# Attention and feed-forward in one kernel: the weight sums moved from the third token tile into the second, with new queue orders

## The chip, the cores and the metric

The kernel runs on one core of a Trainium2 chip. The metric is the time of one execution on the device in microseconds (us); of several runs the median counts. A profile is one further execution, recorded by the hardware.

## What is computed

The input x has 2048 tokens of 512 features. The reference, cut to its core:

```python
xn = _layernorm(x, axis=-1)
q, k, v = (xn @ wqkv).reshape(B, S, 3, H, Dh).transpose(2, 0, 3, 1, 4)      # H = 32, Dh = 16
scores = einsum("bhqd,bhkd->bhqk", q, k) * (Dh ** -0.5)
mask = (i - j >= 0) & (i - j < 256)                                            # sliding window
s = einsum("bhqk,bhkd->bhqd", softmax(where(mask, scores, -1e9)), v).reshape(B, S, D) @ wo
g = silu((silu(xn @ w1) * (xn @ w3)) @ w2)                                     # w1, w3: 512 x 1792
return x + s * g
```

## The kernel before

**Number format.** TensorE multiplies fp16. Each fp32 operand is cut into a high and a low fp16 half (a cast, L1059, and a subtraction, L1060, or the like), and three products of halves stand for one.

**Tiles.** The tokens go in four tiles t = 0 to 3 of 512. The feed-forward part has 14 blocks f of 128 hidden features. For t = 0 and 1, `gate_up` (L1024) multiplies each block by w1 and w3 plainly. For t = 2 and 3 the blocks go in seven pairs j, and `quad(t, j)` makes a pair's 2 x 2 block product with seven multiplications instead of eight, by Strassen's scheme: products p1, p2, p6, p5, p7, p3, p4 in this order, 12 or more matmuls of 256 columns each (L1175). Between them stand pieces of attention, and `down` (L1284), which multiplies by w2.

**What the seven products need.** p1 and p2 take plain weights, which tile 0 left in DRAM as `dW`; p6, p5, p7 and p3 take sums of weight blocks; p6, p5, p7 and p4 take sums of token blocks.

- `weight_sums(j)` makes the sums of pair j, first of w1, then of w3: two loads of 256 KB from HBM (L1073, tensor in_B_w), two scales on ScalarE (L1078), four sums on GpSimd (L1082 to L1085), the cut into halves (L1059, L1060) and two stores of 256 KB to `dSum` (L1094). All seven pairs are made once and are used by both tiles 2 and 3. The pieces are put off by a count of steps (`later`):

```python
for k in range(2):
    n = 8 * k
    later(n, lambda k=k: load(k))
    for i in range(2):
        later(n + 10 + i, lambda i=i, k=k: scale(i, k))
    later(n + 12, lambda k=k: sums(k))
    for i in range(2):
        later(n + 14 + 2 * i, lambda i=i, k=k: cut(i, k))
```

- `token_sums(t)` makes the sums of tile t's tokens on GpSimd (L324, L1125 to L1128), cut into halves in the same way (L1059, L1060).
- `load_quad` brings a pair's plain pieces from `dW` (L1148) and its sums from `dSum` (L1150) back into SBUF, some products ahead of their use.

`QUAD_AT` (L57) says where `feed_forward` starts `weight_sums(j)`: at block f of tile 1, or at pair j of tile 2. `HALVES_AT` (L58) says the same for `token_sums`.

**Behind a product** of a quad: ScalarE copies the bank out (`copied`, L1181) or VectorE adds it to an earlier copy (`added`, L1185); GpSimd multiplies (L1197), ScalarE takes the tangent (L1198), VectorE gates (L1201), and ScalarE and GpSimd cut the result into halves for `down`.

**Attention** in pieces: `pass1` multiplies keys by queries (L652) and VectorE takes row maxima (L665); `pass2` multiplies again (L794), VectorE adds the mask (L800), ScalarE takes the exponential (L802), and TensorE multiplies by the values (L820). `finish` and `normalise` gather the outputs through DMAs (L841, L844, L867, L873) and scale them (L324, L888). `project` makes queries and keys of the next tile (L590, L605, L608, stores L611 to L615), fetched back as KA and qa (L633; the maxima are written into qa by L749).

**What sets the order.** TensorE follows the order in which the code is written. VectorE, ScalarE, GpSimd and SP (which issues nearly all DMAs) follow `QUEUES`: for each engine a list of the numbers of its instructions, laid out by a planner beforehand. `queue` chains them by that list, so each engine runs strictly in this order, and an instruction that waits holds all behind it. `TURNS` adds pairs of a VectorE and a GpSimd instruction of which the first must end before the second starts. Intermediate tiles share 51 slots of SBUF (`take`, `give`), and a new tile waits for the last reader of the old one in its slot. DMAs go out over eight lanes in turn, each waiting for the landing of the one eight places ahead of it.

Of the kernel before, what the change touches and what calls it, by code (L numbers as in the profile page):

```python
# [56 lines left out]
QUAD_AT = ((1, 4), (1, 6), (1, 8), (1, 10), (1, 12), (2, 0), (2, 2))  # L57
# [26 lines left out]
def tile_block(ctx: ExitStack, tc: tile.TileContext, x, wqkv, wo, w1, w3, w2, out):  # L84
# [1302 lines left out]
    def feed_forward():  # L1387

        pieces = []
        late, next_late = [], []  # L1390
        sums_at = dict(zip(QUAD_AT, range(FB // 2)))

# [342 lines left out]
    for n, b in enumerate((1, 3, 0)):  # L1735
# [54 lines left out]
    ),  # L1790
    ENGINE.Activation: (
# [148 lines left out]
```

## Time and profile before

| | |
|---|---|
| median of 3 runs | 793.54 us (793.53 to 795.88) |
| profiled execution, span in it | 799.8 us, 798.0 us |
| granted TensorE clock, mean | 0.998 |
| busy: PE, DVE, ACT, POOL | 779.9, 618.4, 435.1, 398.1 us |
| scales of weights (L1078, 28 of them) | first at 279.0, last at 531.1 us |
| first sums (L1082) of the pairs 0 to 6 | 282.0, 345.7, 356.9, 400.9, 426.0, 458.3 and, of pair 6, after 497.8 us |
| first and last store of sums (L1094) | 288.5 and 561.8 us |
| DMA landing, 256 KB from in_B_w / dW / dSum | 4.5 / 3.8 / 3.6 us after issue (medians) |

Names: PE is TensorE, DVE VectorE, ACT ScalarE, POOL GpSimd, SP or SPq the queue of SyncE; PEld is the loading of weights into TensorE, beside its matmuls. L-numbers are lines of the kernel. A tile's name stands as out<-in: `slot` is any of the 51 tiles, `m` and `s`, `po` are PSUM banks of the feed-forward and of attention, `copy` a quad's copied product, `pt` an exponential. Times count from the span's start. Tile 2 of the feed-forward starts with the first L1181, at 423 us. From 420 to 480 us the queue of SP issues eight loads (L1073) and seven stores (L1094) of 256 KB for the pairs 3 to 5.

### The profile page before, as it was taken

How to read it: one execution, taken by the hardware profiler on the slowest of the kernel's cores; microseconds unless marked ns; L12 is line 12 of the kernel's file. 1: busy time of each engine (PE TensorE's matmuls, PEld its weight loads, DVE VectorE, ACT ScalarE, POOL GpSimd, SP SyncE). 2: the span in 40 equal slices, each digit the busy share in tenths (PEclk: the TensorE clock that was granted, in tenths of full speed). 3: DMA queues.
4: the chain of work that ended last, by engine and by line, in shares of the span. 5: the costliest groups of instructions: out<-in, count | busy, mean ns of one | idle time of the engine just before them, and what ended most of it. 6: DMA issues, size and time to landing. Idle time of an engine off the chain costs nothing.

```text
span 798.0 us, 25742 instructions
## 1 busy us (share of the span) xinstructions
PE 779.9 (98%) x9997; PEld 443.5 (56%) x9997; DVE 618.4 (78%) x2049; ACT 435.1 (55%) x672; POOL 398.1 (50%) x761
## 2 busy tenths in 40 slices
PE   8999999999999999999998789999999999999998
PEld 4444555444455544444446566566666666666654
DVE  8788998777987688777778687767887788876456
ACT  7899768644365444354444466554555445555421
POOL 2264556453323082089996387454883315142451
PEclk9999999999999999999999999999999999999999
DMA  9867672366746545486787875469655666344333
GB/s 305 258 186 254 174 226 69 114 178 226 218 143 187 163 122 142 140 198 204 224 257 220 232 240 154 144 205 269 188 168 179 185 180 180 106 138 139 103 100 121
DMA packets 130123, 144.40 MB, mean 181 GB/s; under 512 B 19472, under 2 KB 87888, under 8 KB 130000
## 3 DMA queue, kind: packets, MB, share of 16 engines
q1 hardware_dynamic: 129712, 142.23, 59.9%
q8 instruction: 78, 1.28, 0.7%
q10 hardware_dynamic: 288, 0.52, 0.2%
q14 instruction: 45, 0.37, 0.2%
HBM read 100.40 MB, written 37.49 MB: 173 GB/s over the span
## 4 chain that ended last, share of the span: by engine, by line
PE 78%; DMA 7%; POOL 4%; DVE 4%; SPq 4%; issue 2%; ACT 1%; DVEq 0%; ACTq 0%; POOLq 0%
PE m L1284 16%; PE m L1024 15%; PE m L1175 14%; PE m L590 8%; PE po L820 7%; PE m L1333 4%; PE s L794 3%; PE m L555 3%; PE s L652 3%; DMA slot<-in_B_w_dram 2%; POOL slot L324 1%; DVE copy L1185 1%; DMA KA<-dK 1%; SPq L749 1%; POOL slot L1060 1%
## 5 line engine op out<-in xcount | busy, mean ns | idle before, releaser
L802 ACT ACTIVATE pt<-s,es 128x1024 f32<-128x1024 f32 x130 | 142.2, 1112 | 75.5 <-DVE s L800 69.7
L1284 PE MATMUL m<-slot,slot 128*128 128x512 f16 x672 | 153.4, 379 | 0.9 <-DVE copy L1185 0.3
L324 POOL TENSOR_TENSOR slot<-slot,slot 128x256 f16<-128x256 f32 (+1 forms) x136 | 91.6, 691 | 121.4 <-ACT slot L1050 56.1
L665 DVE CUSTOM_DVE_ANT_0 junk<-s,MW 128x320 bf16<-128x320 f32 x276 | 127.0, 485 | 12.8 <-PE s L652 5.9
L1024 PE MATMUL m<-XH,slot 128*128 128x512 f16 x448 | 133.6, 380 | 0.0
L1175 PEld LDWEIGHTS <-slot 128*128 128x128 f16 x1176 | 113.0, 98 | 30.3 <-issue 6.0
L800 DVE TENSOR_TENSOR s<-s,MK 128x256 f32<-128x256 f32 (+1 forms) x236 | 99.0, 435 | 38.9 <-PE s L794 34.4
L1284 PEld LDWEIGHTS <-slot 128*128 128x128 f16 x672 | 63.7, 98 | 75.9 <-issue 4.7
L1024 PEld LDWEIGHTS <-slot 128*128 128x128 f16 x672 | 62.9, 98 | 76.3 <-issue 3.5
L1024 PE MATMUL m<-XL,slot 128*128 128x512 f16 x224 | 84.9, 379 | 0.0
L1175 PE MATMUL m<-slot,slot 128*128 128x256 f16 x672 | 81.0, 273 | 3.0 <-DVE copy L1185 1.7
L1197 POOL TENSOR_TENSOR copy<-copy 128x256 f32<-128x256 f32 x56 | 41.4, 743 | 84.6 <-DVE copy L1185 70.9
L665 DVE CUSTOM_DVE_ANT_0 junk<-po,MW 128x320 bf16<-128x320 f32 x172 | 82.1, 483 | 0.0
L820 PE MATMUL po<-pt,V 64*32 64x320 f32 (+4 forms) x2880 | 78.2, 342 | 2.2 <-issue 2.2
L1181 ACT ACTIVATE copy<-m 128x512 f32<-128x512 f32 x56 | 33.4, 597 | 84.5 <-PE m L1175 75.8
L340 POOL TENSOR_TENSOR slot<-slot,slot 128x128 f16<-128x128 f32 x112 | 45.5, 436 | 59.9 <-ACT slot L337 58.9
L590 PE MATMUL m<-XH,slot 128*128 128x512 f16 x240 | 70.7, 380 | 0.2
L820 PEld LDWEIGHTS po<-pt,V 64*32 64x32 f32 x2880 | 53.8, 106 | 21.5 <-issue 3.9
L1175 PE MATMUL m<-XH,slot 128*128 128x256 f16 x336 | 58.0, 277 | 2.8 <-DMA slot<-dW 2.8
L590 PEld LDWEIGHTS <-slot 128*128 128x128 f16 x392 | 36.8, 98 | 41.5 <-issue 1.6
L794 PEld LDWEIGHTS <-KA 50*64 50x64 f16 x1472 | 33.6, 106 | 35.4 <-issue 26.8
L1185 DVE SCALAR_TENSOR_TENSOR copy<-m,copy 128x512 f32<-128x512 f32 x42 | 29.0, 690 | 30.9 <-PE m L1175 30.7
(198 smaller groups left out, 1403.7 us busy)
## 6 DMA issues: line engine op xcount, KB each, us to landing
slot<-dW SPq DMA_DIRECT2D x112, 256.0 KB
slot<-in_B_w_dram SPq DMA_DIRECT2D x70, 256.0 KB
slot<-dSum SPq DMA_DIRECT2D x56, 256.0 KB
dW<-slot SPq DMA_DIRECT2D x42, 256.0 KB
slot<-in_A_x_dram SPq DMA_DIRECT2D x30, 256.0 KB
dSum<-slot SPq DMA_DIRECT2D x28, 256.0 KB
KA<-dK SPq DMA_DIRECT2D x24, 288.0 KB
slot<-dWQ SPq DMA_DIRECT2D x24, 256.0 KB
```

Of the source, the lines that this page charges most:

```text
L324: op(out[:, c], a[:, c], b[:, c])
L340: nc.gpsimd.tensor_sub(lo[:, c // 2, at], raw[:, c * P:(c + 1) * P], hi[:, c // 2, at])
L590: nc.tensor.matmul(cell["pp"][:, cols[n]], w[:, (a * NC + c) * P:(a * NC + c + 1) * P], b[:, c, cols[n]], start=n == 0 and (c, i) == parts ...
L665: nc.vector.tensor_tensor_reduce(out=junk, in0=view, in1=mask, scale=1.0, scalar=NEG, op0=ALU.add, op1=ALU.max, accum_out=M[:, r, a, ii:ii ...
L794: nc.tensor.matmul(s[64 * h:64 * h + 64, r, o:o + 64 * n], ka[rows, 2 * p + a, 64 * (m + 4):64 * (m + 5)], qa[rows, 2 * p + a, 64 * (m + k ...
L800: nc.vector.tensor_add(v, v, MK[:, kind, of:of + n, :].unsqueeze(1).to_broadcast([P, 2 * len(which), n, 64]))
L802: nc.scalar.activation(pt, s, AF.Exp, scale=es)
L820: nc.tensor.matmul(cell["po"][32 * i:32 * i + 32, h, 64 * (m + k):64 * (m + k + n)], V[64 * h:64 * h + 64, (4 * t + m // 2) % VB, hd * VW: ...
L1024: nc.tensor.matmul(cell[k], w[:, at:at + P], b[:, c, :], start=c == 0 and i == 0, stop=c == NC - 1 and i == 2)
L1175: nc.tensor.matmul(ps[:, 256 * k:256 * k + 256], w(k, a, c), x(b, c), start=first and k == 0 and c == 0 and n == 0, stop=k == 1 and c == 1 ...
L1197: nc.gpsimd.tensor_mul(made[:, 256:512], made[:, 0:256], made[:, 256:512])
L1284: nc.tensor.matmul(ps, hh[:, a * TW + b * P:a * TW + (b + 1) * P], w[:, c * D:(c + 1) * D], start=f == f0 and i == 0, stop=f == f1 - 1 and ...
```

## The change

Each pair's sums are started earlier, all within tile 1: pair 0 at its block 1 instead of 4, pair 6 at its block 13 instead of pair 2 of tile 2. `HALVES_AT` stays. The lists of `QUEUES` for all four engines and the pairs of `TURNS` are new throughout, since the numbers of the instructions change with the order of the code. The numbers of instructions are the same.

```diff
-QUAD_AT = ((1, 4), (1, 6), (1, 8), (1, 10), (1, 12), (2, 0), (2, 2))
+QUAD_AT = ((1, 1), (1, 3), (1, 5), (1, 7), (1, 9), (1, 11), (1, 13))
...
 QUEUES = {
     ENGINE.DVE: (
...
-        "0 4 2 1 3 5-9 11 10 12 18-22 13 23-24 14 25 15 26 16 27 17 28-33 35 38 34 37 39 44 40-42 45 47 50 46 48 52-53 "
...
+        "0 4 2 1 3 5 7 6 8-9 11 10 12 18-22 13 23-24 14 25 15 26 16 27 17 28-33 35 38 34 37 39 44 40-42 45 47 50 46 51 "
...
 TURNS = (
-    "240-88 241-90 242-104 255-104 204-104 224-105 205-105 225-105 206-106 226-112 227-94 243-97 244-99 298-122 "
...
+    "198-70 255-108 204-112 205-92 224-113 206-95 243-93 244-97 225-84 227-124 268-125 269-131 271-130 311-148 "
...
```

What the lists do at three places, as the built programs have it. First SP, at the opening of tile 2. Before (`slot_8246` is a plain weight piece of the second quad of tile 2; another, `slot_8141`, stands four rows ahead of these):

```order
L633 DMA qa<-dQ_148 48x4x512 x2
L1150 DMA slot_8265<-dSum 128x1024
L1094 DMA dSum<-slot_7087 128x1024
L1073 DMA slot_7704<-in_B_w_dram 128x4x128
L622 DMA slot_8216<-dWQ 128x1024
L615 DMA dK_153<-slot_8235 128x512
L614 DMA dK_153<-slot_8235 128x2x512
L749 DMA qa<-mt 1x8x128 x2
L844 DMA on<-os 16x512
L749 DMA qa<-mt 1x8x128
L844 DMA on<-os 16x512 x3
L1148 DMA slot_8246<-dW_155 128x2x512
```

Now (the same two pieces are `slot_8319` and `slot_8208`):

```order
L612 DMA dQ_148<-slot_7818 128x512
L873 DMA rb<-de 16x512 x2
L1148 DMA slot_8319<-dW_155 128x2x512
L633 DMA KA_144<-dK_152 48x4x768 x2
L633 DMA qa<-dQ_148 48x4x512 x2
L1148 DMA slot_8208<-dW_155 128x2x512
L841 DMA dr<-os 64x1x32
L1094 DMA dSum<-slot_7525 128x1024
L1094 DMA dSum<-slot_7367 128x1024
L1094 DMA dSum<-slot_7585 128x1024
L1073 DMA slot_7808<-in_B_w_dram 128x4x128
L1150 DMA slot_8335<-dSum 128x1024
```

The piece that stood behind the gathers L844 now stands ahead of the fetches of KA and qa (L633), and the other behind them. The gathers come after all of these rows, and so does the load L1150 that stood next to L633 (on `slot_8265` before, `slot_8337` now).

Second ScalarE, around the first copy of a product in tile 2. Before (slot_7513 and slot_7512 are weights of pair 4):

```order
L802 ACTIVATE pt<-s,es_334 128x1024
L1181 ACTIVATE copy<-m_8030 128x512
L1078 ACTIVATE slot_7513<-slot_7513,inv 128x512
L1078 ACTIVATE slot_7512<-slot_7512,inv 128x512
L1198 ACTIVATE slot_8071<-copy,sga 128x256
L802 ACTIVATE pt<-s,es_334 128x1024 x2
L802 ACTIVATE pt<-po,es_334 128x1024
L1181 ACTIVATE copy<-m_8030 128x512
```

Now (slot_7182 and slot_7181 are weights of pair 5):

```order
L1078 ACTIVATE slot_7182<-slot_7182,inv 128x512
L802 ACTIVATE pt<-s,es_334 128x1024
L1038 ACTIVATE slot_7900<-m_7887,sgs 128x512
L1050 CAST slot_7917<-slot_7900 128x512
L802 ACTIVATE pt<-s,es_334 128x1024
L1078 ACTIVATE slot_7181<-slot_7181,inv 128x512
L1181 ACTIVATE copy<-m_8102 128x512
L802 ACTIVATE pt<-s,es_334 128x1024 x2
L802 ACTIVATE pt<-po,es_334 128x1024
L1181 ACTIVATE copy<-m_8102 128x512
L802 ACTIVATE pt<-s,es_334 128x1024
```

The two scales and the tangent L1198 that stood between the first copy and the exponentials are gone from there; scales of the next pair stand ahead of the copy.

Third VectorE, at the second quad's addition of a product (the last row before, the middle one now). Before:

```order
L665 ISA junk,M<-s,MW 128x320
L665 ISA M 128x1
L665 ISA junk,M<-s,MW 128x320
L665 ISA M 128x1
L665 ISA junk,M<-po,MW 128x320
L665 ISA M 128x1
L513 TENSOR_TENSOR XL<-s,XH 128x2x128
L665 ISA junk,M<-po,MW 128x320
L665 ISA M 128x1
L1185 SCALAR_TENSOR_TENSOR copy<-m_8686,copy 128x512
```

Now:

```order
L665 ISA junk,M<-po,MW 128x320
L665 ISA M 128x1
L665 ISA junk,M<-po,MW 128x320
L665 ISA M 128x1
L464 TENSOR_SCALAR slot_7077<-slot_7077,mv,rs 128x512
L1185 SCALAR_TENSOR_TENSOR copy<-m_8738,copy 128x512
L800 TENSOR_TENSOR s<-s,MK 128x4x64
L665 ISA junk,M<-s,MW 128x320
L665 ISA M 128x1
L800 TENSOR_TENSOR s<-s,MK 128x2x2x64
```

The addition stood behind the masks, the maxima and the cut (L513) of a group of scores; now it stands ahead of them, behind a LayerNorm pass (L464) of tile 3, which came earlier in the list before.

On GpSimd, the cuts of the token sums of tile 2 (L1059, L1060 on `slot_7488` and `slot_7513`, read by p6, p5 and p7) now stand among the last sums and cuts of pair 5, ahead of the first product L1197 of a quad; the sums of pair 4 stood there before. Pair 6 follows behind that L1197, with its loads on SP behind the rows shown.

247 rows, old and new, of tables (QUEUES, TURNS) are left out of this document.

## The prediction

> **What bounds the kernel now.** I read the busy shares first, then TensorE's idle time by stretches, its waits, and the timeline at each place where it stood. First TensorE on the page; then stretches (length, busy time and instructions of PE, PEld, DVE, ACT, POOL, then granted clock, DMA share, GB/s).
> ```profile
> PE 779.9 (98%) x9997; PEld 443.5 (56%) x9997; DVE 618.4 (78%) x2049; ACT 435.1 (55%) x672; POOL 398.1 (50%) x761
> 240.00:340.00 100.00, 99.68 (x1424) 50.73 (x1423) 75.62 (x247) 45.02 (x60) 32.00 (x56) 1.00 0.52 152
> 340.00:420.00 80.00, 79.56 (x974) 38.72 (x979) 59.46 (x200) 39.35 (x49) 75.30 (x132) 1.00 0.77 222
> 420.00:440.00 20.00, 17.93 (x262) 12.51 (x247) 17.25 (x54) 8.79 (x13) 12.52 (x27) 1.00 0.76 215
> 440.00:460.00 20.00, 15.67 (x297) 11.53 (x295) 13.94 (x48) 8.61 (x15) 6.81 (x13) 0.91 0.84 243
> 460.00:480.00 20.00, 17.36 (x351) 11.89 (x349) 16.68 (x50) 12.68 (x23) 16.59 (x27) 1.00 0.73 227
> 520.00:540.00 20.00, 19.14 (x204) 12.58 (x210) 12.77 (x43) 11.46 (x16) 12.40 (x21) 1.00 0.73 213
> ```
> TensorE is the bound, and the change leaves its work as it is: the same rows, but for one group of nine matmuls that changes places with a projection near 385 us. What can be won is idle time. Of 798.0 − 779.9 = 18.1 us, 2.07 + 4.33 + 2.64 = 9.04 lie in 420 to 480, the opening of tile 2, and 0.86 in 520 to 540. The stretch of 440 to 460 also shows a clock of 0.91. From 240 to 420 TensorE was idle for 0.32 + 0.44 = 0.76 us only.
>
> Its waits, by what ended them (total, times, longest):
> ```profile
> PE m L1175 <- DMA slot<-dW: 2.8, 1, 2.8
> PE po L820 <- issue: 2.2, 2, 1.3
> PE m L1175 <- DVE copy L1185: 1.7, 1, 1.7
> PE m L1175 <- ACT V L557: 0.8, 1, 0.8
> ```
> The 2.2 us of "issue" wait for nothing that the profile shows; the other three follow below. All these are of the profiled execution: 799.8 us, 1.8 of it outside the span, and 6.3 above 793.54, the median of the runs. I make the sum in the profiled execution and take the same difference off the median; that some of its stalls may be the profile's own is in the range.
>
> **Place A, 428.7 to 431.3: exponentials late on ScalarE.** TensorE's timeline, then ScalarE's and VectorE's (start, duration, what, idle before):
> ```profile
> 427.26 1.47 PE L1175 MATMUL m<-slot,slot 128*128 128x256 f16 x12
> 429.27 0.42 PE L794 MATMUL s<-qa,KA 50*64 50x320 f16 x12 [0.53 <-ACT pt L802]
> 430.27 0.29 PE L652 MATMUL s<-KA,qa 48*64 48x320 f16 x1 [0.58 <-ACT pt L802]
> 431.28 0.29 PE L652 MATMUL po<-KA,qa 48*64 48x320 f16 x1 [0.71 <-ACT pt L802]
> 425.15 0.72 ACT L1078 ACTIVATE slot<-slot,inv 128x512 f32<-128x512 f32 x1 [1.36 <-DMA slot<-in_B_w_dram]
> 427.10 0.72 ACT L1078 ACTIVATE slot<-slot,inv 128x512 f32<-128x512 f32 x1 [1.22 <-DMA slot<-in_B_w_dram]
> 428.13 2.10 ACT L802 ACTIVATE pt<-s,es 128x1024 f32<-128x1024 f32 x2
> 425.19 1.02 DVE L800 TENSOR_TENSOR s<-s,MK 128x512 f32<-128x512 f32 x2
> ```
> The masks (L800) of the first exponential (L802) were done by 426.2, yet it started at 428.13, behind two scales of pair 4 (L1078) that stood 1.36 + 1.22 us for weights from HBM. TensorE lost 0.53 + 0.58 + 0.71 = 1.82. The change takes these scales, and the tangent behind them, out of the way: after the first L1181 the exponentials come next, up to 1.9 us earlier, which covers each gap. I take 1.5 (0 to 1.8; a scale of pair 5, on slot_7181, now stands one place ahead of L1181 and can itself be late).
>
> **Place C, 449.0 to 455.5: a weight piece for the second quad's next product.** The load's issue, its flight in the chain of waits, and TensorE's restart:
> ```profile
> 444.55 2.47 SPq L844 DMA_DIRECT2D on<-os  x3
> 447.12 4.95 DMA slot<-dW
> 452.12 0.60 PE L1175 MATMUL m<-XH,slot 128*128 128x256 f16 x2 [2.82 <-DMA slot<-dW]
> 452.12 2.74 PE m L1175 x12
> 464.59 1.47 PE L1175 MATMUL m<-slot,slot 128*128 128x256 f16 x12 [1.72 <-DVE copy L1185]
> 434.26 0.87 SPq L633 DMA_DIRECT2D KA<-dK  x2
> ```
> The 256 KB landed 4.95 us after issue, and the issue stood behind three gathers (L844). Twelve matmuls then took 2.74 us, where others take 1.47: half clock. A clock of 0.91 over 20 us is 0.09 × 20 / 0.5 = 3.6 us at half speed, so at most 1.8 us of work is lost by it; I take 1.4 (at least the 2.74 − 1.47 = 1.27 shown). In the new SP order this load stands ahead of the fetches of KA and qa (L633), so it goes out before 434.3 and lands by 439.2, ten microseconds ahead of use. Gain 2.8 + 1.4 − 0.2 for new neighbours = 4.0 (2.5 to 4.5).
>
> The Trainium skill ("TensorE: Matmul & The Clock Gate", Part 1: The HAM clock gate) says that the clock falls to half after an idle window of some 3.4 us and comes back after as long a stretch of work. The trace agrees in the half and roughly in the length (3.6), but it fell after gaps of 1.34 and 2.82 us, neither of them so long. By the rule a new stall under 3.4 us would cost nothing beside itself; by the row it can cost 1.27 more, which is what I use.
>
> **Place D, 462.9 to 464.6: 1.72 us for one VectorE addition** (L1185), which stood behind masks, a cut and row maxima (L665, 485 ns below):
> ```profile
> 463.11 0.42 DVE L513 TENSOR_TENSOR XL<-s,XH 128x256 f16<-128x256 f32 x1
> 463.85 0.69 DVE L1185 SCALAR_TENSOR_TENSOR copy<-m,copy 128x512 f32<-128x512 f32 x1
> L464 DVE TENSOR_SCALAR slot<-slot,mv,rs 128x512 f32<-128x512 f32 x16 | 8.5, 566 | 0.0
> ```
> It now stands ahead of two masks (0.5 each, from 1.02 for two), four maxima and the cut: 1.0 + 1.9 + 0.4 = 3.3 us less of VectorE ahead of it; two passes L464 put in front take back 1.1. That covers 1.72: gain 1.4 (0 to 1.7).
>
> **Place E, 531.6 to 532.4: 0.8 us** behind two scales of pair 6:
> ```profile
> 530.47 1.34 ACT L1078 ACTIVATE slot<-slot,inv 128x512 f32<-128x512 f32 x2 [1.29 <-DMA slot<-in_B_w_dram]
> ```
> These scales now stand among ScalarE's rows of 440 to 485. Gain 0.8 (0.5 to 0.9). The two gaps of "issue" I leave as they are: 0. Together 1.5 + 4.0 + 1.4 + 0.8 = 7.7 us.
>
> **What the move costs.** The work of the pairs is not less, only earlier. Prices of its parts on GpSimd (345 to 420):
> ```profile
> L1060 POOL TENSOR_TENSOR slot<-slot,slot 128x256 f16<-128x256 f32 x32 | 21.2, 671 | 0.5
> L1059 POOL CAST slot<-slot 128x256 f16<-128x256 f32 x32 | 12.5, 396 | 0.1
> L1082 POOL TENSOR_TENSOR slot<-slot 128x256 f32<-128x256 f32 x6 | 4.3, 724 | 0.3 <-ACT slot L1078 0.3
> ```
> A pair is 8 sums of 0.724, 8 casts of 0.396 and 8 subtractions of 0.671: 14.3 us, and 8 transfers of 256 KB. Three pairs were made after 420; now six are cut ahead of the first tangent's product (L1197, 431.26 below), so GpSimd takes on about two pairs, 28.7 us, in 240 to 431. Its row of 32.00 in 100 us shows room early; 75.30 of 80 shows none late. TensorE doesn't see early work as long as no operand it needs is cut late.
>
> One such operand I can place: the token sums for product 6 of the first quad, read from 427.26 on (place A). GpSimd's timeline, and the row of SP's queue near which a weight load is now issued:
> ```profile
> 415.25 1.92 POOL L324 TENSOR_TENSOR slot<-slot,slot 128x256 f16<-128x256 f32 x3
> 417.83 2.56 POOL L1060 TENSOR_TENSOR slot<-slot,slot 128x256 f16<-128x256 f32 x4
> 425.95 0.73 POOL L1082 TENSOR_TENSOR slot<-slot 128x256 f32<-128x256 f32 x1 [5.56 <-ACT slot L1078]
> 431.26 0.72 POOL L1197 TENSOR_TENSOR copy<-copy 128x256 f32<-128x256 f32 x1
> 415.36 1.40 SPq L749 DMA_DIRECT2D qa<-mt  x2
> ```
> Before, GpSimd had them by 420.4 and then stood idle. Now the last of them is cut behind three of the four last sums of pair 5. From the second of the three L324, near 415.9, to that cut's end are 17 instructions of 0.39 to 0.73, 10.6 us: 426.5 if no load is late. But the last load of pair 5 stands in SP's new order just ahead of the qa writes of 415.36; issued near 415 and landing 3 to 6 us later (4.95 at C), it holds the sums, behind which 6.7 us are left, until 419 to 422: cut at 426 to 429. Cost 0 to 2 us, taken 0.7.
>
> A load of sums for the second quad (L1150) stood on SP at 436.20, and now stands ten DMAs later, behind the gathers:
> ```profile
> 436.20 0.39 SPq L1150 DMA_DIRECT2D slot<-dSum  x1
> ```
> That is near 445, landing near 450; use was at 455 (after C's twelve) and comes near 449 when A and C are gone: 0 to 2, taken 0.7. Another weight piece on SP (L1148, slot_8208) now waits for GpSimd to be done with pair 5, with everything behind it on SP; it is read only after 440: 0 to 1, taken 0. In 240 to 420 the scales of two more pairs stand in ScalarE's queue ahead of exponentials, as at A: each late load can cost what A cost, 1.8, or nothing, and the idle 0.76 us of that stretch says that the slack there was ample: 0 to 4, taken 0.8. The costs sum to 2.2.
>
> Does a busier GpSimd slow VectorE? Row maxima with GpSimd at 32 of 100, then at 75.3 of 80 us:
> ```profile
> L665 DVE CUSTOM_DVE_ANT_0 junk<-s,MW 128x320 bf16<-128x320 f32 x44 | 20.2, 485 | 5.0 <-ACT XH L508 3.8 <-PE s L652 1.2
> L665 DVE CUSTOM_DVE_ANT_0 junk<-s,MW 128x320 bf16<-128x320 f32 x38 | 17.7, 486 | 2.9 <-PE s L652 2.9
> ```
> By 1 ns: cost 0. The Trainium skill ("SBUF — State Buffer", SBUF: two separate sides) speaks against the change here: a VectorE instruction with two SBUF inputs and one of GpSimd lock each other out. The maxima read one operand from PSUM, so these rows don't test it; by the rule each L1328 (two tiles in SBUF) between 240 and 420 could wait up to 0.7 us, and the sum would change by tenths, since it stands on no wait above.
>
> **The sum:** 7.7 − 2.2 = 5.5 us: 794.3 for a profiled execution, 788.0 as the median.
>
> **Rivals.**
> - Almost all is won: costs come to 0.5, and one gap of "issue" (1.3) goes, with fewer transfers beside it. 7.7 + 1.3 − 0.5 = 8.5: 785.0, at best 782. For it: 420 to 480 loses some seven of fifteen transfers for sums, and 14 us on GpSimd. Against it: "issue" names no transfer. Chance 0.23.
> - No change; the wait only changes its place. Product 6 waits 2 for its token sums, L1150 is 2 late, early scales cost 0.8, C gains its low end 2.5 and D nothing: 1.5 + 2.5 + 0.8 − 4.8 = 0: 793.5, within the 2.4 us (0.3%) that a measurement of this kernel can tell from no change. For it: GpSimd at 75.3 of 80 ahead of product 6. Chance 0.14.
> - Slower: GpSimd falls behind before 427. The two pairs more fit only into the early room (68 us idle in 240 to 340); if loads and free slots let less than half of the 28.7 us be done there, 14 us are late at 427. TensorE stands for them, less the 5.6 us that GpSimd idled at 420 to 426, plus 1.3 of clock: 9.7 lost against 7.7 won, 795.5. It decides from some 12 us of lateness. Against it: a fifth of that room is enough. Chance 0.12.
> - My forecast, a gain of 2.4 to 8: chance 0.51, alone 785.5 to 791.
>
> The range takes in the first rival's end, 782.0, and the slower one's 795.5. Faster 0.74, same 0.14, slower 0.12.
>
> **What will show it.** Right: no wait of L1175 on slot<-dW and a clock of 1.00 in 440 to 460 (C); L802 within 0.5 us of its masks near 426 (A); no L1175 wait on L1185 near 463 (D); no L1078 near 530 (E); some 6 us more of TensorE busy in 420 to 480. Wrong: L1175 waiting for GpSimd's L1060 near 427 or for dSum near 450, or more than 2 us of idle TensorE in 240 to 420, where ScalarE or GpSimd would stand for an early load.

## The result and the profile after

| | before | after |
|---|---|---|
| median | 793.87 us (5 runs, 793.53 to 798.16) | 788.40 us (5 runs, 788.05 to 788.87) |
| ratio | | 0.9917, 95% interval 0.9891 to 0.9943 |
| profiled execution, its span | 799.8, 798.0 us | 788.5, 786.7 us |
| TensorE busy, rest of the span | 779.9, 18.1 us | 777.8, 8.9 us |

The change gains 5.5 us (6.5 against 794.9, the median of 35 further runs of the kernel before). It does something else besides: the five runs after lie within 0.8 us of each other, while 102 further runs of the kernel before lay between 792.0 and 800.4. The granted clock alone is not the gain: of those 102, the 53 with a mean clock of 0.999 or 1.000 still took 794.5 us in the median. The ratios below are those on record with their 95% intervals; they are not the quotients of the two medians and can differ from these by up to 0.14%.

The same stretches and waits of TensorE after (columns as in the prediction), with one stretch of before that was not shown, the last of the five:
```profile
240.00:420.00 180.00, 180.00 (x2430) 90.40 (x2436) 136.29 (x453) 90.59 (x118) 132.73 (x233) 1.00 0.68 202
420.00:440.00 20.00, 19.76 (x262) 13.55 (x251) 17.97 (x60) 10.15 (x14) 14.41 (x32) 1.00 0.88 263
440.00:460.00 20.00, 18.84 (x394) 14.55 (x378) 18.34 (x60) 11.36 (x20) 10.32 (x17) 1.00 0.70 220
460.00:480.00 20.00, 19.73 (x359) 14.32 (x358) 16.05 (x52) 14.47 (x22) 14.85 (x25) 1.00 0.55 165
500.00:560.00 60.00, 59.06 (x768) 37.12 (x766) 44.07 (x148) 32.39 (x46) 29.64 (x49) 1.00 0.68 204
...
PE po L820 <- issue: 0.6, 1, 0.6
PE s L794 <- ACT pt L802: 0.5, 1, 0.5
PE m L1175 <- DVE slot L608: 0.2, 1, 0.2
```
In 420 to 480 the idle time fell from 9.04 to 0.24 + 1.16 + 0.27 = 1.67 us, the clock is 1.00 throughout, and of the four waits that the prediction took up, three are gone and the gap of issue is 0.6 instead of 2.2. From 240 to 420, where GpSimd now works for 132.7 us instead of 107.3, TensorE has no idle time at all.

The places one by one after: ScalarE, VectorE and TensorE at A; SP's issue of C's weight piece; GpSimd's cut of the token sums, and their first use (the row of 426.26); SP's late load of sums (L1150):
```profile
424.96 2.13 ACT L802 ACTIVATE pt<-s,es 128x1024 f32<-128x1024 f32 x2 [2.18 <-DVE s L800]
424.18 1.02 DVE L800 TENSOR_TENSOR s<-s,MK 128x512 f32<-128x512 f32 x2
427.66 0.42 PE L794 MATMUL s<-qa,KA 50*64 50x320 f16 x12
427.09 0.42 SPq L1148 DMA_DIRECT2D slot<-dW  x1
423.15 1.29 POOL L1060 TENSOR_TENSOR slot<-slot,slot 128x256 f16<-128x256 f32 x2
426.26 1.47 PE L1175 MATMUL m<-slot,slot 128*128 128x256 f16 x12
444.32 0.43 SPq L1150 DMA_DIRECT2D slot<-dSum  x1
```
The exponentials now wait for their masks and for nothing else. The weight piece goes out 20 us earlier than at 447.12. The last token sum is cut at 424.4, 1.8 us ahead of use. L1150 goes out at 444.3, as worked out, and no matmul waits for dSum.

### The profile page after: what moved, and what is told of

Same layout as the page of the kernel before. It is cut to its first block, busy times and chain, and to the rows that moved or that the text cites. A ratio compares the mean times of both kernels' runs of the same rounds, so it can differ in the third digit from the quotient of the medians.

```text
span 786.7 us, 25767 instructions
## 1 busy us (share of the span) xinstructions
PE 777.8 (99%) x9997; PEld 443.5 (56%) x9997; DVE 615.3 (78%) x2049; ACT 435.9 (55%) x672; POOL 399.0 (51%) x761
## 4 chain that ended last, share of the span: by engine, by line
PE 94%; DVE 3%; ACT 2%; issue 1%; DMA 1%; SPq 0%; DVEq 0%; ACTq 0%
PE m L1284 19%; PE m L1024 19%; PE m L1175 15%; PE m L590 9%; PE po L820 9%; PE m L555 5%; PE m L1333 5%; PE s L652 4%; PE s L794 4%; DVE copy L1185 1%; ACT pt L802 1%; PE po L652 1%; PE s L500 1%; PE s L590 1%; DMA slot<-in_A_x_dram 1%
## 5 line engine op out<-in xcount | busy, mean ns | idle before, releaser
L802 ACT ACTIVATE pt<-s,es 128x1024 f32<-128x1024 f32 x130 | 142.4, 1112 | 85.1 <-DVE s L800 77.0
L1175 PEld LDWEIGHTS <-slot 128*128 128x128 f16 x1176 | 112.6, 98 | 24.0 <-issue 3.7
L1197 POOL TENSOR_TENSOR copy<-copy 128x256 f32<-128x256 f32 x56 | 41.8, 749 | 101.6 <-DVE copy L1185 89.4
L1175 PE MATMUL m<-slot,slot 128*128 128x256 f16 x672 | 80.9, 273 | 0.5 <-DVE slot L608 0.2
L820 PE MATMUL po<-pt,V 64*32 64x320 f32 (+4 forms) x2880 | 77.7, 342 | 0.6 <-issue 0.6
L820 PEld LDWEIGHTS po<-pt,V 64*32 64x32 f32 x2880 | 54.1, 106 | 19.0 <-issue 1.7
L1175 PE MATMUL m<-XH,slot 128*128 128x256 f16 x336 | 56.9, 273 | 0.0
```

Source lines behind the costliest of these rows:

```text
L802: nc.scalar.activation(pt, s, AF.Exp, scale=es)
L820: nc.tensor.matmul(cell["po"][32 * i:32 * i + 32, h, 64 * (m + k):64 * (m + k + n)], V[64 * h:64 * h + 64, (4 * t + m // 2) % VB, hd * VW: ...
L1175: nc.tensor.matmul(ps[:, 256 * k:256 * k + 256], w(k, a, c), x(b, c), start=first and k == 0 and c == 0 and n == 0, stop=k == 1 and c == 1 ...
L1197: nc.gpsimd.tensor_mul(made[:, 256:512], made[:, 0:256], made[:, 256:512])
```

## The experiments

Numbers in the lists of `QUEUES` are those of the instructions in code order. Each kernel ran beside the kernel before on the same chip.

### A second profile of the kernel before

No edit. 

> The kernel before, unchanged, once more with a profile. Its profiled execution took 799.8 us, 6.3 above its median, while that of the changed kernel took 788.5, its median. Theory 1: most executions of the kernel before lack a part of the stalls of 420 to 480 us (the half clock, the two gaps of issue), and a profile of such an execution shows a span near 792, a clock of 1.00 in 440 to 460 and 3 to 6 us less idle TensorE in 420 to 480. Theory 2: the profile itself lengthens this kernel, and the span is near 798 again with the same gaps.

Measured: 795.92 us in the median of 12 (794.28 to 798.87); the profiled execution took 795.9. Stretches and gaps of TensorE in 420 to 480:
```profile
420.00:440.00 20.00, 19.50 (x244) 13.28 (x241) 18.33 (x57) 10.59 (x15) 14.09 (x31) 1.00 0.78 213
440.00:460.00 20.00, 15.51 (x304) 11.90 (x286) 14.98 (x49) 10.29 (x18) 8.45 (x14) 0.91 0.73 221
460.00:480.00 20.00, 18.98 (x354) 12.56 (x354) 16.16 (x48) 13.67 (x23) 17.32 (x30) 1.00 0.69 216
...
444.93 0.88 PE L820 MATMUL po<-pt,V 64*32 64x128 f32 x28 [2.31 <-issue]
449.43 0.39 PE L1175 MATMUL m<-XH,slot 128*128 128x256 f16 x2 [0.98 <-DMA slot<-dW]
460.75 1.47 PE L1175 MATMUL m<-slot,slot 128*128 128x256 f16 x12 [1.72 <-DVE copy L1185]
```
The stalls are not the same ones. Place A, 1.82 us in the first profile, is gone (0.50 us idle in 420 to 440); C's wait is 0.98 instead of 2.82, the gap of issue 2.31 instead of 1.34; D's 1.72 is the same. Theory 1 holds in part: there are 3.0 us less idle time in 420 to 480, but the half clock stays, and the span is 794.1 us, not near 792. The 799.8 us of the first profile were one end of a spread, and which place stalls changes from one execution to the next.

### One place mended at a time

```diff
 A, Activation: ... 359
-353 351 360-363
+360-363 353 351
 ... 364
 C, SP: ... 561 551 573
+572
 ... 557-560 574 ... 552-554
-572
 ... 564; load_quad(2, 1, 1) gets a tile of its own, and cpool 6 buffers instead of 7
 D, DVE: ... 958
+977
 ... 978-981 983 982 984
-977
 ... 994
```
C needs the tile of its own: its slot of SBUF holds halves that two stores (L614 and L615 in the SP rows ahead of the prediction) still read until 445.7 us, so moved alone it would wait on SP for stores that stand behind it. The smaller ring of copies has a run of its own below.

A: 

> The kernel before, with the two scales of pair 4 moved behind the three exponentials on ScalarE (place A alone). Theory 1, the terms of the prediction add up: 1.5 us faster (792.0). Theory 2, A's gain is swallowed: TensorE then comes earlier to the weight piece of place C, which lands at the same time, so the wait there grows by what A gave and the time stays within 0.5 us of 793.5.

C: 

> The kernel before, with the weight piece of place C issued ahead of the fetches of KA and qa, into a tile of its own (its slot is in use until a store lands near 445.7); to make room for it the ring of copies has 6 tiles instead of 7. Theory 1 (place C costs 2.8 us and 1.4 of half clock in every execution): 4 us faster, 789.5, no wait on slot<-dW. Theory 2 (a typical execution pays the wait but no half clock): 2.5 to 2.8 faster, 791. Theory 3: next waits (row maxima, sums) take it back: under 1 us.

D: 

> The kernel before, with VectorE's addition of place D moved ahead of the masks and maxima of its group of scores (place D alone). Theory 1: 1.4 us faster, 792.1. Theory 2: the maxima that are now 0.7 us later hold a later product as long, and the time stays within 0.5 us of 793.5.

Measured: A 795.97 us, ratio 1.0011 (0.9994 to 1.0027); C 795.04, 0.9994 (0.9976 to 1.0011); D 795.48, 0.9999 (0.9981 to 1.0017); before 794.92 (35 runs). None gains anything that can be told. The intervals exclude the prediction's 1.5 us for A and 4.0 for C; for D they reach a gain of 1.5, so that its 1.4 is not excluded. TensorE's gaps, A first, then C, then D (A's profiled execution took 798.5 us, near the top of its twelve):
```profile
443.72 0.68 PE L500 MATMUL s<-identf,slot 64*32 64x64 f32 x32 [2.62 <-DVE slot L464]
471.10 1.96 PE L820 MATMUL po<-pt,V 64*32 64x320 f32 x40 [2.12 <-issue]
...
445.69 0.55 PE L820 MATMUL po<-pt,V 64*32 64x128 f32 x28 [1.89 <-issue]
452.40 0.41 PE L794 MATMUL s<-qa,KA 50*64 50x320 f16 x8 [1.01 <-ACT pt L802]
459.87 1.47 PE L1179 MATMUL m<-slot,slot 128*128 128x256 f16 x12 [1.72 <-DVE copy L1189]
...
448.59 0.39 PE L1175 MATMUL m<-XH,slot 128*128 128x256 f16 x2 [2.87 <-DMA slot<-dW]
465.20 0.33 PE L652 MATMUL s<-KA,qa 48*32 48x320 f16 x8 [0.76 <-ACT pt L802]
```
(In C's kernel and the later ones with its tile, lines behind 1144 are four further down.) Each mended wait is gone from its own profile (A's was gone from the second profile of before as well), and TensorE stands elsewhere: at L464 and issue with A mended, at issue and L802 with C, at C's load, as before, and newly at L802 with D. By the times, theory 2 holds for A and D and theory 3 for C. The mechanism expected for A does not: C's wait did not grow, it is not in that profile, and L464 came in its place.

The control for the ring: 

> The kernel before with the ring of copies of 6 tiles instead of 7, nothing else: the control for the early weight piece, which needed that room and came out at 795.0 beside 794.9 before. Theory 1 (the waits of 420 to 480 stand one behind the other, and taking away one only lengthens the next): no difference, within 1 us of before. Theory 2 (the smaller ring costs what the early piece gives): 2 us or more slower.

Measured: 794.01 us, 0.9991 (0.9976 to 1.0006). The smaller ring costs nothing, so it did not hide a gain of C.

### The four places at once, and a fifth

```diff
 A, C and D as above
 E, Activation: ... 443
-423 421 444-445
+444-445 423 421
```


> The kernel before with places A, C, D and E mended at once in its own order of sums: the two scales of pair 4 behind the exponentials, the weight piece early in a tile of its own (6 copies in the ring), the addition ahead of its masks, the two scales of pair 6 behind L557. Theory 1 (the four terms of the prediction, 7.7 us, are the gain, whatever makes them): 787 to 789. Theory 2 (the loads and stores of the pairs in 420 to 480 make TensorE late in ever new places, and only their removal helps): 793 or more, with the gap of issue near 444 still 1 to 2.5 us and waits for L464 or L802 in place of those mended.

Measured: 795.46 us, 1.0010 (0.9994 to 1.0026). That is theory 2's time, with its wait for L464; the gap of issue that it named near 444 is missing (0.4 us at 468 is all). TensorE's gap, then GpSimd's rows that lead to it, then VectorE's:
```profile
443.78 0.68 PE L500 MATMUL s<-identf,slot 64*32 64x64 f32 x32 [3.26 <-DVE slot L464]
429.22 0.73 POOL L1082 TENSOR_TENSOR slot<-slot 128x256 f32<-128x256 f32 x1 [9.45 <-ACT slot L1078]
438.71 1.31 POOL L1060 TENSOR_TENSOR slot<-slot,slot 128x256 f16<-128x256 f32 x2
439.97 0.21 POOL L452 TENSOR_TENSOR sq<-r 128x4 f32<-128x4 f32 x1
442.57 0.20 POOL L461 TENSOR_TENSOR rs<-sq,r 128x4 f32<-128x4 f32 x1
442.81 1.79 DVE L464 TENSOR_SCALAR slot<-slot,mv,rs 128x512 f32<-128x512 f32 x2 [3.62 <-POOL rs L461]
```
GpSimd makes the scale of tile 3's LayerNorm (L452 to L461) behind the sums and cuts of pair 4, and these wait for the scales that A moved back. What ScalarE gave to the exponentials, GpSimd lost, and TensorE's transposes (L500) paid 3.3 us for it. This is no rare execution: all twelve show a mean clock below 0.999, as only 49 of the 102 of the kernel before do. So the way in which A is mended costs something itself, and this run doesn't show what C, D and E would give without it. Hence the next edit, which takes pair 4's sums out of GpSimd's way too:
```diff
 A, C, D and E as above
 G, Pool: ...
-473-474 485 475 483 486 484 497 476 422 421 458 457 460 459 477 479 478 480 461-470
+497 422 421 458 457 460 459 461-470 473-474 485 475 483 486 484 476 477 479 478 480
```


> The kernel before with A, C, D and E mended as in the run that came out at 795.5, and with the twelve GpSimd instructions of pair 4's first half (L1082 to L1085 and the cuts, 7.9 us) moved behind the chain L452 to L461. That chain gives the LayerNorm of tile 3 (L464), for which TensorE's transposes (L500) waited 3.3 us in that run. Theory 1 (GpSimd's queue at the opening of tile 2 was the fifth wait, hidden behind the others): the wait at L500 is gone and the time is 788 to 790. Theory 2 (late landings find ever new places as long as the pairs' transfers run there): 792 or more.

Measured: 800.24 us, 1.0060 (1.0034 to 1.0086): slower, outside both theories. TensorE's gap, then SP's and GpSimd's rows behind it:
```profile
450.83 0.64 PE L794 MATMUL s<-qa,KA 50*64 50x256 f16 x8 [5.77 <-DMA qa<-mt]
430.90 0.92 SPq L633 DMA_DIRECT2D qa<-dQ  x2
440.36 0.34 SPq L1154 DMA_DIRECT2D slot<-dSum  x1
439.01 1.31 POOL L1060 TENSOR_TENSOR slot<-slot,slot 128x256 f16<-128x256 f32 x2
```
The wait at L500 is gone, as theory 1 had it. But the next load of sums (L1150, here L1154) goes into slot 38, in which pair 4's raw weights lie until GpSimd has cut them at 440.3. SP stood for it from 431.8 to 440.4, and the maxima that it writes into qa behind it came 5.8 us late. So in this order pair 4 can't go earlier, its loads land too late, and it can't go later, its slots are needed. The new plan has it out of the way altogether.

### Lighter loads and sums, in the old order

```diff
+                n = 1 if j in (4, 5) else NC
-                nc.sync.dma_start(raw.rearrange("p (c f) -> p c f", f=P),
-                                  w[:, f * P:(f + 1) * P].rearrange("(c p) f -> p c f", p=P))
+                nc.sync.dma_start(raw.rearrange("p (c f) -> p c f", f=P)[:, 0:n, :],
+                                  w[:, f * P:(f + 1) * P].rearrange("(c p) f -> p c f", p=P)[:, 0:n, :])
...
             raw = cell[k][i]
-            nc.scalar.activation(raw, raw, AF.Copy, scale=inverses[:, j, k, i:i + 1])
+            src, dst = raw, raw
+            if j in (4, 5):
+                src = identf.unsqueeze(1).to_broadcast([P, NC, P])
+                dst = raw.rearrange("p (c f) -> p c f", f=P)
+            nc.scalar.activation(dst, src, AF.Copy, scale=inverses[:, j, k, i:i + 1])
...
             a, b = cell[k]
+            w = 16 if j in (4, 5) else 256
+            l, r = slice(0, w), slice(256, 256 + w)
```
The first of three kernels has the loads light, the second the sums too (the last two lines), and the third the places A, C, D, E and G besides. The first:

> The kernel before with the sixteen loads... of pairs 4 and 5 (eight of them, L1073, in 420 to 470 us) cut to a quarter of their bytes, 64 KB each; their scales read a constant instead, so these two pairs' sums are not those of the weights. Order, instructions and waits stay. Theory 1 (bytes in flight between 420 and 470 make the landings late: A's scales, C's piece, instruction fetches): 3 us or more faster, 790 to 792, and the runs lie closer together. Theory 2 (it is the order of the queues and the slots, not the bytes): within 1 us of before.

(Eight loads are meant.) Measured: 793.23 us (791.14 to 798.57), 0.9993 (0.9974 to 1.0011).

The second: 

> The kernel before with the eight loads of pairs 4 and 5 at a quarter of their bytes (as before, their scales read a constant) and their sixteen GpSimd sums (L1082 to L1085) on 16 columns instead of 256, so that these pairs' sums are not those of the weights. Order and waits stay. Theory 1 (bytes and GpSimd time between 420 and 470 are what the change removes, and what it gains by): 789 to 791. Theory 2 (order and slots alone bind, since the light loads alone gave at most 1.6 us): 792.5 or more, with the gaps at L1185 and L464 as before.

Measured: 793.67 us (790.53 to 798.75), 0.9986 (0.9964 to 1.0008).

The third: 

> Both at once: the five places mended in the order before, and the loads and sums of pairs 4 and 5 light (their sums are not those of the weights). Theory 1 (places and loads together are all of the change's gain): 787.5 to 789, runs within 1.5 us of each other as those of the changed kernel. Theory 2 (something else in the new plan gives a part, in 0 to 420 or after 500): 790 or more.

Measured: 797.78 us, 1.0033 (1.0017 to 1.0050).

For the first two, theory 2 holds: neither the bytes of pairs 4 and 5 nor the time of their sums on GpSimd give the change's 5.5 to 6.5 us. A part of it is not excluded: the medians lie 1.6 and 0.9 us below those of the kernel before (794.83 and 794.53), and the intervals allow gains up to 2.1 and 2.9. With both light, TensorE still waited 2.32 us for C's piece and 1.7 at D (its line 1182 is L1175); the last line is of the third kernel:
```profile
446.42 0.61 PE L1182 MATMUL m<-XH,slot 128*128 128x256 f16 x2 [2.32 <-DMA slot<-dW]
...
PE m L1182 <- DVE copy L1192: 1.7, 1, 1.7
...
PE s L794 <- DMA qa<-mt: 3.9, 1, 3.9
```
The third run does not test its theory 1. It holds edit G, which alone had made the kernel slower, and SP stood again for the slot that G keeps in use, from 432.9 to 440.0, so the maxima in qa came 3.9 us late. Light loads and sums took 2.5 us off the run with G (800.24 to 797.78). A, C, D and E with light loads and without G were not run.

### The changed kernel with one part put back

C's piece late on SP:
```diff
 SP: ... 505 503
-582
 ... 569-573 564 ... 576-577
+582
 ... 584
```


> The changed kernel with the weight piece of place C (L1148, slot_8319) issued 31 DMAs later on SP, behind the writes of qa near 443.6 us, so that it lands near 448.5 where TensorE wants it at 445.3. Theory 1 (a wait of 3 us on an otherwise gapless TensorE costs itself and a half clock behind it, as the profile of before showed): 3.2 + 1.4 = 4.6 slower, 793.0, clock 0.91 in 440 to 460. Theory 2 (the wait alone, clock 1.00): 3.2 slower, 791.6. Theory 3 (later work has slack that gives it back): under 1 us slower.

(It is 23 DMAs.) Measured: 790.51 us in the median of 12, from 788.48 to 795.28; 0.9954 (0.9935 to 0.9973) against before. Slower by 2.1 in the median, between theories 2 and 3, for in the profiled execution, which is the fastest, SP had reached the load by 442.0 and the wait was short:
```profile
442.00 0.45 SPq L1148 DMA_DIRECT2D slot<-dW  x1
445.06 0.39 PE L1175 MATMUL m<-XH,slot 128*128 128x256 f16 x2 [0.28 <-DMA slot<-dW]
```
What this run shows is the spread. One load issued just in time, in a plan with few other gaps, turned five runs within 0.8 us of each other into twelve runs 6.8 us apart. The granted clock of each run is on record and splits them: the six at 0.999 or 1.000 took 788.5 to 790.6 us, the six at 0.996 to 0.998 took 790.4 to 795.3. So a half clock, as in theory 1, came in some executions and not in others; where in the span it came, a mean doesn't say. That the landing's own scatter decides it is the likely reading; the slow executions have no profile.

Half a pair of sums back into the opening:
```diff
 Pool: ... 388
-493 485 494 507 505 495 506 508 486-487 497 488 498 496 501 503 502 504 533
+485-487 497 488 498 533 493-494 507 505 495 506 508 496 501 503 502 504
 ... 454
```


> The changed kernel with one half pair of sums put back to where GpSimd made sums before: the twelve instructions of pair 5's second half (L1082 to L1085, their cuts L1059 and L1060, 7.9 us) are moved from ahead of the first L1197 to behind it, into the opening of tile 2. Nothing else is moved. Theory 1 (the change gains because GpSimd's queue, and through the slots SP's, is free at the opening): GpSimd reaches L452 near 439 instead of 435, L464 comes 4 us later and TensorE's L500 waits some 3 us; the weight piece in the slot of these sums and all behind it on SP go out 4 to 5 us later; 3 to 6 us slower than the changed kernel, 791.5 to 794.5, and its runs spread by over 2 us. Theory 2 (the gain comes from the four places A, C, D and E by their order alone, with GpSimd off the path): under 1 us slower, 788 to 789.4.

Measured: 788.96 us in 4 runs (788.51 to 789.04), 0.9913 (0.9897 to 0.9930) against before: theory 2's time. GpSimd's first and last row of the half pair, and the start of the LayerNorm chain:
```profile
424.99 0.73 POOL L1082 TENSOR_TENSOR slot<-slot 128x256 f32<-128x256 f32 x1
430.47 1.31 POOL L1060 TENSOR_TENSOR slot<-slot,slot 128x256 f16<-128x256 f32 x2
435.60 0.20 POOL L452 TENSOR_TENSOR sq<-r 128x4 f32<-128x4 f32 x1 [0.51 <-DVE r L437]
```
Eight us of sums in the opening cost nothing that can be told: 788.96 against 788.40 us, measured in different series, and 0.9913 against 0.9917 of the kernel before. The weights were there: GpSimd did these sums from 425.0 to 431.8 without a wait and still stood for VectorE (L437) before L452. In the kernel before it idled 5.56 us for pair 4's scales ahead of such work. This points to the wait for loads issued at 421, and not to GpSimd's work at the opening; half a pair is all that was put back. Theory 2's cause, the four places by their order alone, does not follow from its time: mended in the old order they gained nothing.

### What follows

In the kernel before, weights issued at 421 met an opening in which ScalarE, GpSimd, SP and the slots were each close to holding TensorE. Shown are: that the places A, C and D one by one, and all four with E, give no gain in the old order that can be told; that lighter transfers and sums give, by their interval, 2.9 us at most; that mending A moves the wait to L464 through GpSimd, and mending that moves it to SP through a slot; and that with the loads early, a half pair of sums at the opening is nearly free. Not tried are C, D and E without A, the four places with light loads and without G, the old plan with its loads alone issued earlier, and the new places with late sums; the last two need queue orders planned anew. What makes the gain of the new plan, the earlier sums or the rest of it, therefore stays open.

## Why the prediction was right, and where it wasn't

The time, 788.0 against 788.4, and the side were right. The way there was right in part.

- **Places A, C, D, E.** All four waits are gone from the profile after, with the half clock, as said. But the step "together 1.5 + 4.0 + 1.4 + 0.8 = 7.7 us" took them as terms that stand by themselves and come in every execution. In the second profile of the kernel before A's wait was absent and C's was 0.98 us, so A's and C's terms were sized by one execution at the slow end. Mended one by one or together in the old order they give nothing that can be told: mending A makes GpSimd late, and another wait comes in its place.
- **C's cause.** The step "the issue stood behind three gathers" named the nearer half. The slot, held by stores until 445.7, bound it as well, and the change helped by giving the piece another slot (slot 2, free by 427).
- **The gaps of issue.** "I leave as they are: 0" was mis-sized: 2.2 became 0.6, so 1.6 us more.
- **The costs.** "The costs sum to 2.2" was mis-sized: they were 0. The token sums were cut at 424.4 (worked out: 426 to 429), L1150 went out at 444.3 and nothing waited for it, and TensorE's idle time in 240 to 420 went from 0.76 to 0.00 instead of growing by 0.8. GpSimd had no idle load to wait for ahead of the cut, so the risk on which the two cautious rivals stood didn't come to bear.
- **The base.** "Take the same difference off the median" was the weakest step. The profiled execution moved by 799.8 − 788.5 = 11.3 us, twice the 5.5 of the sum: 9.2 us of idle time (7.4 in 420 to 480, 0.8 in 240 to 420, 0.6 in 500 to 560, 0.5 in the first 20) and 2.1 of busy time, most of it half clock. The 794.3 us given for a profiled execution was 5.8 too high. But the execution of before that was profiled lay 6.3 above its median, and the median moved by 5.5. Too small a gain and too slow a base cancelled; that the forecast came within 0.4 us of the result is luck.

The half clock went with its waits, as the step had it; it was priced at 1.4, and TensorE's busy time fell by 2.1. The gap of 1.34 us, which the prediction named beside C's, had no part in it (last section).

## What to carry to other kernels

Where a tuned kernel's bound engine shows several short waits close together on different releasers, they are probably ends of parallel chains with little slack, and their sum is gained only by a change that relieves the chains; mending one wait shows the next. A load issued a few microseconds ahead of its use cost 2.1 us in the median here and much more in the spread, so move it early, and check whose slot it needs. Compare profiles with the median first, and profile the kernel before twice: a spread of 1% between its executions says that the one profile's stalls are not the typical ones.

## What was not expected of the hardware

- **Instruction fetch.** The gap of issue at L820 came in most profiles, and by the trace's packet records TensorE resumed 1.25 to 1.46 us after a 16 KB packet of the instruction queue had landed (before: landed 446.02, resumed 447.33; its second profile 443.63 and 444.93; C mended 444.45 and 445.69; D mended 442.47 and 443.76; after 442.01 and 443.47). It stands where some 130 short matmuls (L500, L820) run in 2.9 us, and is long where the packet starts late. What makes it start late wasn't tried.
- **Half clock after short gaps.** The clock of 440 to 460 was 0.91 after gaps of 1.34 and 2.82 us, 2.31 and 0.98, 1.00 and 2.87, 2.62 alone, and 3.26 alone, but 1.00 after 1.89, 0.23 and 1.01. The clock records of the fourteen profiles say why. Before the last few microseconds of the span, half speed lasts 3.41 us or twice that wherever it comes, and starts a whole number of 3.41 us after the first record. Cut into windows by this grid, up to 786 us, half speed followed every window in which TensorE was idle for 1.84 us or more (twelve windows, up to 3.25), and none with up to 1.83, but for two windows in or right behind a stretch of half speed (1.37 and 1.68). So a single gap is enough if it falls into one window: 2.13 us of C's 2.82 in the first profile, 2.23 of the gap of issue in the second, 2.11 at 469.0 to 471.1 with A mended. The 1.89 us with C mended lay across two windows, 0.56 and 1.33, and cost no clock. The grid stands elsewhere against the program in each profile, so the same gap may cost half clock in one execution and not in the next. The Trainium skill ("TensorE: Matmul & The Clock Gate", Part 1: The HAM clock gate) speaks of an idle window of some 3.4 us; the length agrees with these rows, but the window was not idle throughout.
